# Attention plus channel-mixer block on one core: the load of the next head group's value weights is named after a unit's query stack pieces, its split one step later

## The chip, the cores and the metric

One Trainium2 chip, one of its cores. The metric is the device time of one execution of the whole program in microseconds (us). Three timed executions of the kernel before stand beside one that was profiled.

## The reference, cut to what matters

The input is 2048 tokens of width 1024, in float32. The first half of the block is a layer norm, an attention with 32 heads of width 32 that works through the sequence in four segments of 512 tokens with a running memory M, z, and a residual. The second half is a layer norm, a 1024 to 3584 to 1024 GELU network per token and another residual.

```
q, k, v = y @ wq, y @ wk, y @ wv            # y = layernorm(x), split into 32 heads, 4 segments
for s in range(4):
    p     = softmax(qs @ ks.T * scale + mask)
    a_dot = p @ vs
    a_mem = (phi(qs) @ M) / (phi(qs) @ z + 1e-6)
    o     = g * a_mem + (1 - g) * a_dot
    M, z  = M + phi(ks).T @ vs, z + sum(phi(ks))
h   = x + concat(o) @ wo
out = h + gelu(layernorm(h) @ w1 + b1) @ w2 + b2
```

## The kernel before, in words

Every product is made of float32 values split into a high part and a low remainder (`mm3`, lines 126 to 129: high by high, low by high, high by low), so a weight block comes from HBM as float32, is copied by VectorE or ScalarE to its high part, and GpSimd subtracts to give the low part.

The program runs twice over a half of 1024 tokens (two segments); the attention of each half comes first, the output projection and the mixer follow. The attention (`attention`, line 360) is cut into 16 **units** per half: a unit is one group of four heads (128 of the 1024 columns, so eight groups) and one segment. `ORDER` (lines 31 and 32) says which: groups 0 and 1 alternate in units 0 to 3, groups 2 to 5 take two units each, groups 6 and 7 alternate in units 12 to 15. The next unit has another head group after units 0, 1, 2, 3, 5, 7, 9, 11, 12, 13 and 14, and then its three weight blocks (q, k, v, of 512 KB each) must be fetched and split.

**Steps.** A unit is 24 steps, numbered from b = 24n. At step c TensorE does three matmuls of the unit's own projection: keys at c = 0 to 7, queries at 8 to 15, values at 16 to 23. After these, `close(step)` (line 678) runs the functions that were named for that step by `at(step, ...)`: in the order in which they were entered for it. A unit reaches over several later units: its logits start at step 22 (`QK1`, line 37), its second pass at 53, its product with the values at 71. The whole attention is recorded under `in_order()` (line 107), so each engine's instructions stand in exactly the order in which the steps name them, on SyncE's queue of transfers too. When an instruction must wait, all behind it on that engine wait as well.

**The stack pieces.** The logits need the high and low parts of four heads stacked on the partitions, (`stack`, line 414): three transfers of 64 KB for each of four heads j, for keys into `ks`, for queries into `qs`, all of them issued by SyncE. For the queries, ScalarE makes the high part `qq` at step b+15 (line 434), VectorE the low part at b+16 (line 440), and the pieces for j = 0 and 1 are named at b+17, for j = 2 at b+19, for j = 3 at b+24 (there right after the keys of j = 3). The first logits matmul of a unit (`qk1`, line 569) stands at b+22 and needs the three pieces of j = 0. VectorE reads its output (line 571), ScalarE takes the exponential one step later (line 573), and two PSUM banks take turns. "Query pieces 0 to 2" below are the nine transfers of j = 0, 1 and 2.

**The weights.** `wload` (lines 685 to 689) takes one of two raw buffers `wr` and issues the 512 KB load from SyncE (line 688). `wsplit` (lines 691 to 704) has VectorE copy the block to `wh` (line 695), and enters four pieces for the four steps behind it, in which GpSimd makes `wl` (line 699). The buffer is free when the fourth piece is done. Since there are two buffers, the load of v takes the one that k had in the same unit, and the next load of a k, q or v takes what is free. In units 1 to 14 that fetch weights the loads stand at b+2 (k), b+7 (q; b+13 in unit 1) and b+15 (v), the splits at b+9, b+17 and b+25.

Also on GpSimd in these steps: the causal cut of the exponentials `e` (line 626, `qk2`, named from step 53 on, which is b+5 to b+20 of a later unit and b+29 and on as seen from here), and the low part of the attention output (line 654, step 75).

Of the kernel before, what the change touches and what calls it, by code (L numbers as in the profile page):

```python
# [51 lines left out]
def build(tc, x, wq, wk, wv, wo, beta, w1, b1, w2, b2, out):  # L52
# [6 lines left out]
    def ps_dense(name):  # L59
        return psum.tile([P, 512], F32, tag="d", name=name, bufs=3)  # L60
# [16 lines left out]
    def constants():  # L77
        behind(nc.scalar.activation(bb, bb, AF.Exp, scale=-1.0))
        nc.scalar.activation(bb, bb, AF.Identity, bias=1.0)
        behind(nc.vector.reciprocal(gate[:, 0, :], bb))  # L80
        nc.scalar.activation(gate[:, 1, :], gate[:, 0, :], AF.Identity, scale=-1.0, bias=1.0)
        pb = ps_dense("pb")
        behind(nc.tensor.transpose(pb[:, :FB], b1r, ident[:FB, :FB]))
        nc.scalar.copy(b1c, pb[:, :FB])
        for j in range(4):
            b = slice(32 * j, 32 * j + 32)
            nc.gpsimd.tensor_copy(gcol[b, :], gate[b, 1, :].rearrange("p (g j) -> p g j", j=4)[:, :, j])
# [38 lines left out]
    def mm3(ps, ah, al, bh, bl, first, last):  # L126
        nc.tensor.matmul(ps, ah, bh, start=first, stop=False)  # L127
        nc.tensor.matmul(ps, ah, bl, start=False, stop=False)  # L128
        acts["mm"] = nc.tensor.matmul(ps, al, bh, start=False, stop=last)  # L129
# [230 lines left out]
    def attention(half, first):  # L360
# [15 lines left out]
        def at(step, *fns):  # L376
            assert step >= now[0], (step, now[0])
            todo.setdefault(step, []).extend(fns)
# [281 lines left out]
        def heads(u, b):  # L660
            for m, (j, i) in QK1.items():
                at(b + m, partial(qk1, u, j, i))
            at(b + QK0, partial(qk0, u))
            at(b + LSE, partial(lse, u))
            at(b + LSE + 1, partial(halves, u))
            at(b + TURN, partial(turn, u))
            for j, m in enumerate(ROWS):
                at(b + m, partial(rows, u, j))
            for m, (j, n) in QK2.items():
                at(b + m, partial(qk2, u, j, n))  # L670
            at(b + AV, partial(av, u))
            at(b + AV + 2, partial(out, u))
            at(b + AV + 3, partial(out_high, u))
            at(b + AV + 4, partial(out_low, u))
            if u["n"] < 13:
                at(b + AV + 6, partial(store, u))

        def close(step):

            now[0] = step  # L680
            for f in todo.pop(step, ()):
                f()
            one_small()
# [35 lines left out]
        for n in range(16):  # L719
            u = unit(n)  # L720
            heads(u, 24 * n)
            g, sl = ORDER[n]
            b = 24 * n
            if n < 15 and ORDER[n + 1][0] != g:
                g1 = ORDER[n + 1][0]
                for name, m, m1 in (("k", 2, 9), ("q", 7 if n > 1 else 13, 17), ("v", 15, 25)) if n else \
                        (("k", 14, 19), ("q", 17, 24), ("v", 24, 32)):
                    at(b + m, partial(wload, g1, name))
                    at(b + m1, partial(wsplit, g1, name, step=b + m1))
            if n == 14:  # L730
                for k, m in enumerate((1, 4, 8, 25, 27, 29, 41)):
                    at(b + m, partial(load_o, half, 0, k))
            if n == 15:
                wts, raws = acts["wts"], acts["raws"] = {}, {}

                def wo_load(k):
                    raws[0, k] = wo_raw(0, k)

                def wo_made(k, step):
                    wts[0, k], lows_ = wo_upper(raws.pop((0, k)), wo_home())  # L740
                    for i, f in enumerate(lows_):
                        at(step + 1 + i, f)

                for m, k in ((6, 0), (7, 1), (17, 2), (22, 3)):
                    at(b + m, partial(wo_load, k))
                for m, k in ((12, 0), (17, 1), (24, 2)):
                    at(b + m, partial(wo_made, k, b + m))
            acc = 0.0
            for c in range(24):
                name = "kqv"[c // 8]  # L750
                if c % 8 == 0:
                    u[name + "ps"] = ps_dense(name + "ps") if not (first and n == 0 and c == 0) else first["kps"]
                if first and n == 0 and c < 8:
                    if c == 7:
                        close(b + c)
                    continue
                w = first[name] if first and n == 0 else W[g, name]
                yh, yl = acts["y", sl]
                k = c % 8
                mm3(u[name + "ps"], w[0][:, k, :], w[1][:, k, :], yh[:, k, :], yl[:, k, :], k == 0, k == DC - 1)  # L760
                close(b + c)
                if side:
                    acc += 0.55 if half else 0.7
                    while acc >= 1.0:
                        acc -= 1.0
                        next(side, None)
            if n == 1:
                for _ in side:
                    pass
                side = None  # L770
                if first:
                    constants()
                acts.pop("last", None)
# [25 lines left out]
    def wo_raw(n, k):  # L799
        wr = wp.tile([P, DC, P], F32, tag="wr", name="wr", bufs=2).rearrange("p a b -> p (a b)").rearrange("p (c n) -> p c n", c=2)  # L800
        nc.sync.dma_start(wr, wo[k * 256:(k + 1) * 256, n * 512:(n + 1) * 512].rearrange("(c p) n -> p c n", p=P))
        return wr
# [6 lines left out]
    def wo_upper(wr, home):  # L809
        h, l = home  # L810
        nc.vector.tensor_copy(h, wr)

        def lower(i, c):
            c = slice(256 * c, 256 * c + 256)
            nc.gpsimd.tensor_tensor(l[:, i, c], wr[:, i, c], raw(h)[:, i, c], op=ALU.subtract)

        return home, [partial(lower, i, c) for i in range(2) for c in range(2)]

    def wo_home():
        return [wp.tile([P, DC, P], F32R, tag=t, name=t, bufs=3).rearrange("p a b -> p (a b)")  # L820
                .rearrange("p (c n) -> p c n", c=2) for t in ("wh", "wl")]
# [615 lines left out]
    for half in range(2):  # L1437
# [6 lines left out]
        order = ExitStack()  # L1444
        order.enter_context(in_order())
        rest = attention(half, first)
        next(rest)
        hts = [lnp.tile([P, D], F32, tag="ln", name="ht0", bufs=4) for _ in range(4)]
# [125 lines left out]
```

## Time and profile before

| | us |
|---|---|
| timed executions | 2183.11, 2184.59, 2187.11 |
| their median | 2184.59 |
| the profiled execution, its own time | 2187.23 |
| its span, first to last instruction | 2185.5 |
| TensorE busy in the span | 2157.7 |
| VectorE, ScalarE, GpSimd busy | 1349.0, 1102.1, 959.7 |

The profiled execution ran at the full granted TensorE clock. How to read it: a busy time is the sum of an engine's instructions, and an engine waits when an instruction that is next in its order needs something. A row of the timeline gives the start, the duration, the engine and line, what is written from what, and in brackets the idle time before it and who ended that. SPq is SyncE's queue, where a transfer's row is only its issue. Its landing is told by the view of transfers. Matmul rows overlap: a 128x512 matmul has about 0.39 us in the record, and the next may start 0.23 us after it started.

### The profile page before, as it was taken

To read this page: it belongs to the slowest core of one execution; us is meant where nothing else is said; L and a number is where in the kernel's file an instruction comes from. 1 tells how busy PE (TensorE), PEld (TensorE's weight loads), DVE (VectorE), ACT (ScalarE), POOL (GpSimd) and SP (SyncE) were. 2 spreads that over 40 slices of the span, in tenths; PEclk is the share of its full clock that TensorE was granted. 3 is DMA by queue.
4 is the path that set the end of the run, shared out by engine and by line. 5 is a ranking of instruction groups with operands and counts; after the bars stand their busy time and mean duration, and the time that the engine had idled before them with its cause. 6 is when DMAs were issued, how large, how long until landed. Compare 5 with 4: busy or idle time off the path is not lost.

```text
span 2185.5 us, 33210 instructions
## 1 busy us (share of the span) xinstructions
PE 2157.7 (99%) x10937; PEld 1750.4 (80%) x10937; DVE 1349.0 (62%) x2696; ACT 1102.1 (50%) x2433; POOL 959.7 (44%) x1206
## 2 busy tenths in 40 slices
PE   7999999999999999999999999999999999999999
PEld 6777777778888888877777768888887888888887
DVE  6766666665745556766667655745666665576653
ACT  5777777762543445777777752643443232322221
POOL 5534345562444434533335561534446544256330
PEclk9999999999999999999999999999999999999999
DMA  6544445664465655544444663575569865676762
GB/s 182 134 106 107 105 107 136 190 203 164 154 207 155 187 158 147 136 107 109 106 108 133 198 197 141 173 217 162 171 199 373 274 226 185 190 244 230 250 222 92
DMA packets 352405, 376.20 MB, mean 172 GB/s; under 512 B 27214, under 2 KB 244330, under 8 KB 352234
## 3 DMA queue, kind: packets, MB, share of 16 engines
q1 hardware_dynamic: 288778, 336.98, 50.7%
q10 hardware_dynamic: 63456, 37.10, 5.6%
q8 instruction: 87, 1.43, 0.3%
q14 instruction: 84, 0.69, 0.1%
HBM read 241.27 MB, written 82.38 MB: 148 GB/s over the span
## 4 chain that ended last, share of the span: by engine, by line
PE 91%; DVE 2%; DMA 2%; POOL 2%; ACT 1%; issue 1%; SPq 0%; ACTq 0%; DVEq 0%; POOLq 0%
PE po L1410 22%; PE bps L1014 10%; PE cps L1014 7%; PE dps L1014 7%; PE pst L619 4%; PE po L633 3%; PE pqk L569 3%; PE kps L127 3%; PE vps L127 3%; PE qps L127 3%; PE kps L128 3%; PE pwo L127 2%; PE kps L129 2%; PE vps L128 2%; PE pwo L129 2%; PE pwo L128 2%
## 5 line engine op out<-in xcount | busy, mean ns | idle before, releaser
L571 DVE CUSTOM_DVE_ANT_0 pqk<-pqk,mask 128x512 f32<-128x512 f32 (+2 forms) x384 | 216.9, 565 | 241.6 <-PE pqk L569 214.8
L573 ACT ACTIVATE junk<-pqk,mx 128x512 f32<-128x512 f32 (+2 forms) x384 | 225.2, 587 | 134.7 <-DVE mx L571 128.2
L626 POOL TENSOR_SCALAR_AFFINE_SELECT e<-e 128x128 f32<-128x128 f32 (+1 forms) x384 | 137.6, 359 | 268.9 <-ACT e L622 254.1
L699 POOL TENSOR_TENSOR wl<-wr,wh 128x256 fp32r<-128x256 f32 x268 | 202.1, 770 | 108.7 <-PE pqk L569 85.8
L622 ACT ACTIVATE e<-pst 128x384 f32<-128x384 f32 (+1 forms) x384 | 200.8, 529 | 70.9 <-PE pst L619 69.5
L1420 DVE TENSOR_TENSOR c<-c,po 128x512 f32<-128x512 f32 x160 | 105.4, 684 | 156.7 <-PE po L1410 153.9
L569 PE MATMUL pqk<-ks,qs 96*128 96x512 f32 (+2 forms) x384 | 138.6, 361 | 5.7 <-ACT junk L573 3.0
L619 PE MATMUL pst<-qs,ks 104*128 104x512 f32 (+3 forms) x512 | 140.9, 318 | 1.0 <-ACT e L622 0.4
L619 PEld LDWEIGHTS pst<-qs,ks 104*128 104x128 f32 x512 | 95.7, 188 | 34.7 <-ACT e L622 10.7
L1410 PE MATMUL po<-w2h,zh 128*128 128x512 f32 x378 | 120.9, 389 | 0.4 <-DVE zh L1350 0.4
L1267 POOL TENSOR_TENSOR w2r<-w2r 128x512 f32<-128x512 f32 x54 | 84.6, 1579 | 72.3 <-DMA w2r<-in_B_w 72.3
L127 PE MATMUL kps<-yh,wh 128*128 128x512 f32 (+1 forms) x264 | 113.5, 430 | 0.0
L127 PE MATMUL qps<-yh,wh 128*128 128x512 f32 x256 | 113.2, 442 | 0.0
L1014 PE MATMUL bps<-zh,sb 128*128 128x512 f32 x336 | 110.9, 391 | 0.0
L1014 PE MATMUL bps<-zh,sa 128*128 128x512 f32 x336 | 110.8, 390 | 0.0
L1126 POOL TENSOR_TENSOR s<-r 128x512 f32<-128x512 f32 x28 | 44.3, 1583 | 141.0 <-DVE sa L1142 81.3
L127 PE MATMUL vps<-yh,wh 128*128 128x512 f32 x256 | 105.0, 410 | 0.0
L1410 PE MATMUL po<-w2h,hl 128*128 128x512 f32 x322 | 103.2, 390 | 0.7 <-DVE hl L1350 0.4
L128 PE MATMUL kps<-yl,wh 128*128 128x512 f32 (+1 forms) x264 | 102.8, 389 | 0.5 <-DVE yl L165 0.4
L129 PE MATMUL kps<-yh,wl 128*128 128x512 f32 (+1 forms) x264 | 102.2, 387 | 0.0
L128 PE MATMUL qps<-yl,wh 128*128 128x512 f32 x256 | 101.0, 394 | 0.0
L128 PE MATMUL vps<-yl,wh 128*128 128x512 f32 x256 | 100.8, 394 | 0.0
(271 smaller groups left out, 6204.0 us busy)
## 6 DMA issues: line engine op xcount, KB each, us to landing
hr<-h_dram SPq DMA_DIRECT2D x112, 448.0 KB, 5.5
w2r<-in_B_w SPq DMA_DIRECT2D x122, 256.0 KB, 4.2
r<-in_B_w SPq DMA_DIRECT2D x56, 512.0 KB, 4.6
ks<-kk SPq DMA_DIRECT2D x360, 64.0 KB, 2.0
qs<-qq SPq DMA_DIRECT2D x360, 64.0 KB, 2.0
h_dram<-ht ACTq DMA_DIRECT2D x84, 256.0 KB, 3.6
wx<-in_B_w SPq DMA_DIRECT2D x56, 256.0 KB, 3.5
o_dram<-side SPq DMA_DIRECT2D x52, 256.0 KB, 4.2
```

Source lines behind the costliest of these rows:

```text
L127: nc.tensor.matmul(ps, ah, bh, start=first, stop=False)
L128: nc.tensor.matmul(ps, ah, bl, start=False, stop=False)
L129: acts["mm"] = nc.tensor.matmul(ps, al, bh, start=False, stop=last)
L569: nc.tensor.matmul(ps, u["qs"][0:96, j, i * P:(i + 1) * P], u["ks"][0:96, j, 0:n], start=True, stop=True)
L571: nc.vector.tensor_tensor_reduce(out=ps, in0=ps, in1=mask[:, 512 - n:512], op0=ALU.add, op1=ALU.min, scale=-SCALE, scalar=3.0e38, accum_out=m)
L573: at(now[0] + 1, lambda: nc.scalar.activation(acts["junk"][:, :n], ps, AF.Exp, bias=m, scale=-1.0, accum_out=u["mx"][:, 1, i, j:j + 1]))
L619: nc.tensor.matmul(ps[:, o:o + 512 - P * jk], u["ks"][:, j, jk * P:(jk + 1) * P], u["qs"][:, j, jk * P:512], start=True, stop=True)
L622: nc.scalar.activation(e, ps[:, :w], AF.Exp, scale=SCALE)
L626: nc.gpsimd.affine_select(d, d, pattern=[[0, 2], [1, P]] if n == 2 else [[1, P]], compare_op=ALU.is_ge, fill=0.0, base=0, channel_multipli ...
L699: nc.gpsimd.tensor_tensor(l[:, c], wr[:, c], raw(h)[:, c], op=ALU.subtract)
L1014: nc.tensor.matmul(ps, x_[:, c, :], y_[:, c, :], start=first and c == 0 and n == 0, stop=last and c == 3 and n == 2, skip_group_check=True)
L1410: nc.tensor.matmul(ps, x_[:, k], y_[k], start=opens and k == 0 and i == 0, stop=closes and k == self.KP - 1 and i == 2, skip_group_check=True)
```

## The change: what it does

The load of v moves from step b+15 to b+21, and its split from b+25 to b+26, in units 1 to 14 where the next unit has another head group: 10 units per half (1, 2, 3, 5, 7, 9, 11, 12, 13, 14), 20 in all. Unit 0, which has its own steps, stays.

```diff
             if n < 15 and ORDER[n + 1][0] != g:
                 g1 = ORDER[n + 1][0]
-                for name, m, m1 in (("k", 2, 9), ("q", 7 if n > 1 else 13, 17), ("v", 15, 25)) if n else \
+                for name, m, m1 in (("k", 2, 9), ("q", 7 if n > 1 else 13, 17), ("v", 21, 26)) if n else \
                         (("k", 14, 19), ("q", 17, 24), ("v", 24, 32)):
                     at(b + m, partial(wload, g1, name))
                     at(b + m1, partial(wsplit, g1, name, step=b + m1))
```

Three engines get another order. On SyncE's queue the load of v (`wr<-in_A_wv`) stood ahead of the query pieces of its unit, in the fence below in a unit of the first half:

```order
 L688 DMA wr<-in_A_wq 128x8x128
 L417 DMA ks_179<-kk 32x512 x6
-L688 DMA wr<-in_A_wv 128x8x128
 L417 DMA qs_181<-qq 32x512 x6
 L417 DMA ks_179<-kk 32x512 x3
 L417 DMA qs_181<-qq 32x512 x3
+L688 DMA wr<-in_A_wv 128x8x128
 L417 DMA ks_179<-kk 32x512 x3
 L417 DMA qs_181<-qq 32x512 x3
```

It now stands behind the query pieces of j = 0, 1 and 2 and the key pieces of j = 2: twelve transfers later, ahead of the pieces of j = 3.

On VectorE the copy to the high part (`wh<-wr`, line 695) moves behind one logits tile (line 571, two rows), in a unit whose two-unit-older neighbour has its output scaled just ahead (line 644):

```order
 L571 ISA mx 128x1
 L644 TENSOR_SCALAR side<-po,few 128x512
-L695 CAST wh<-wr 128x1024
-L571 ISA pqk,mx<-pqk,mask 128x256
-L571 ISA mx 128x1
+L571 ISA pqk,mx<-pqk,mask 128x256
+L571 ISA mx 128x1
+L695 CAST wh<-wr 128x1024
 L469 SCALAR_TENSOR_TENSOR rg<-pm,bb 128x2x4
 L472 RECIPROCAL rg<-rg 128x2x4
```

It now stands right ahead of the reads of the memory product (lines 469 and 472), and the logits tile of step b+26 no longer stands behind it.

On GpSimd the four pieces of v's low part (`wl<-wr,wh`, line 699) each stand one step later. Before, in a stretch that starts with the last three pieces of q's and the first of v's:

```order
L699 TENSOR_TENSOR wl<-wr,wh 128x256 x4
L654 TENSOR_TENSOR side<-side 128x512
L699 TENSOR_TENSOR wl<-wr,wh 128x256 x2
L626 AFFINE_SELECT e<-e 128x128
L699 TENSOR_TENSOR wl<-wr,wh 128x256
L626 AFFINE_SELECT e<-e 128x128
L626 AFFINE_SELECT e<-e 128x256
```

And now, the same stretch:

```order
L699 TENSOR_TENSOR wl<-wr,wh 128x256 x3
L654 TENSOR_TENSOR side<-side 128x512
L699 TENSOR_TENSOR wl<-wr,wh 128x256 x2
L626 AFFINE_SELECT e<-e 128x128
L699 TENSOR_TENSOR wl<-wr,wh 128x256
L626 AFFINE_SELECT e<-e 128x128
L699 TENSOR_TENSOR wl<-wr,wh 128x256
L626 AFFINE_SELECT e<-e 128x256
```

The attention output's low part (line 654) goes ahead of all four of v's pieces, and the fourth goes behind one more cut of `e`. TensorE and ScalarE keep their order.

## The prediction

> **What bounds the kernel now.** I read the page first, then who TensorE waits for, then SyncE's own waits and the view of transfers, and last the timeline around the two waits. The page's first part and the line on TensorE's waits:
>
> ```profile
> PE 2157.7 (99%) x10937; PEld 1750.4 (80%) x10937; DVE 1349.0 (62%) x2696; ACT 1102.1 (50%) x2433; POOL 959.7 (44%) x1206
> ...
> PE pqk L569 <- DMA qs<-qq: 2.4, 2, 1.3
> ```
>
> TensorE is the bound, 99% busy, and other engines have slack. What this change can win must be idle time of TensorE that ends with query stack pieces: 2.4 us, in two waits, the longest 1.3 us. SyncE's queue waits far more at the weight loads (line 688), for GpSimd, and transfers to landing have very different lengths:
>
> ```profile
> SPq L688 <- POOL e L626: 70.5, 25, 3.7
> SPq L688 <- POOL wl L699: 20.9, 13, 3.8
> ...
> qs<-qq SPq DMA_DIRECT2D x360, 64.0 KB, 2.0
> ...
> wr<-in_A_wv SPq DMA_DIRECT2D x24, 512.0 KB, 4.3
> ```
>
> A stack piece lands 2.0 us after its issue at the median, a v block 4.3. In time order, here is the first of the two waits (unit 1 of the first half):
>
> ```profile
> 56.02 0.59 ACT L434 CAST qq<-qps 128x512 fp32r<-128x512 f32 x1 [1.49 <-PE qps L129]
> 57.56 0.69 DVE L440 TENSOR_TENSOR qq<-qps,qq 128x512 fp32r<-128x512 f32 x1
> 58.19 0.37 SPq L688 DMA_DIRECT2D wr<-in_A_wv  x1
> 58.66 3.71 SPq L417 DMA_DIRECT2D qs<-qq  x6
> 61.84 0.40 PE L129 MATMUL vps<-yh,wl 128*128 128x512 f32 x1
> 63.52 0.47 PE L569 MATMUL pqk<-ks,qs 96*128 96x512 f32 x1 [1.28 <-DMA qs<-qq]
> ```
>
> The high part `qq` was done at 56.61, but the pieces were issued only from 58.66, behind a v load that SyncE could not issue before 58.19. The second (unit 7):
>
> ```profile
> 221.54 0.39 PE L129 MATMUL vps<-yh,wl 128*128 128x512 f32 x1
> 221.61 0.58 ACT L434 CAST qq<-qps 128x512 fp32r<-128x512 f32 x1
> 221.77 0.39 PE L569 MATMUL pqk<-ks,qs 96*128 96x512 f32 x1
> 221.86 0.39 SPq L688 DMA_DIRECT2D wr<-in_A_wv  x1
> 222.34 5.05 SPq L417 DMA_DIRECT2D qs<-qq  x6
> 222.82 0.69 DVE L440 TENSOR_TENSOR qq<-qps,qq 128x512 fp32r<-128x512 f32 x1
> 226.85 0.39 PE L129 MATMUL vps<-yh,wl 128*128 128x512 f32 x1
> 228.37 0.47 PE L569 MATMUL pqk<-ks,qs 96*128 96x512 f32 x1 [1.13 <-DMA qs<-qq]
> ```
>
> Here the issue was only 0.14 us behind `qq` (222.19 to 222.34); the transfers were late. The view of transfers for this stretch, and the landings of these pieces (shortest, median, longest):
>
> ```profile
> wr<-in_A_wv SPq DMA_DIRECT2D x1, 512.0 KB, 4.6
> qs<-qq SPq DMA_DIRECT2D x6, 64.0 KB, 4.0
> ...
> DMA to landing us min/median/max: 3.4/4.0/4.5
> ```
>
> Pieces behind a v block take 4.0 us instead of 2.0: they wait for it on the transfer engines. Most units have about 2 us to spare there, which is why only two of the 20 moved places show a wait.
>
> **The change part by part.** *The load leaves the pieces' way.* In unit 1 they can be issued from 56.61, the third piece (the low part, ready at 58.25) at about 58.3; with 2.0 us they land by 60.3, before TensorE comes to them at about 62.1. In unit 7 the third is issued when the low part is done (223.51), and with the longest landing of 4.5 it was there at about 228.0; with the median of 2.0 it is there at 225.5, and TensorE comes at 227.1 (226.85 and 0.23). Both waits go. In starts of matmuls: from a line-129 matmul to a logits matmul it is 0.23 us where nothing waits (221.54 to 221.77); it was 1.68 (61.84 to 63.52) and 1.52 (226.85 to 228.37). So 1.45 + 1.29 = 2.74 us go, a little more than the idle record, because records of matmuls overlap. What is late next in unit 7 is nothing: the windows from the first logits matmul of one unit to that of the next, which end at the moved units 7 (with the wait at 228.37) and 9 (without one; the second figure is TensorE's busy time),
>
> ```profile
> 200.40:228.40 28.00, 26.80 (x158) 20.96 (x156) 17.11 (x50) 20.68 (x58) 11.60 (x23) 1.00 0.49 130
> 256.40:283.00 26.60, 26.54 (x157) 21.05 (x156) 16.52 (x50) 19.94 (x55) 10.79 (x21) 1.00 0.52 138
> ```
>
> show 26.80 of 28.00 and 26.54 of 26.60. A moved unit without such a wait has next to nothing to give, and nothing else idles near unit 7 that would take back what is won.
>
> *The load issues later.* It now follows twelve pieces. The place is where the pieces of j = 3 start, in unit 3 at 120.25:
>
> ```profile
> 112.17 0.39 SPq L688 DMA_DIRECT2D wr<-in_A_wv  x1
> ...
> 120.25 3.02 SPq L417 DMA_DIRECT2D ks<-kk  x3
> 123.49 0.69 DVE L695 CAST wh<-wr 128x1024 fp32r<-128x1024 f32 x1
> 124.16 0.43 DVE L571 CUSTOM_DVE_ANT_0 pqk<-pqk,mask 128x256 f32<-128x256 f32 x1
> 125.01 1.29 POOL L654 TENSOR_TENSOR side<-side 128x512 fp32r<-128x512 f32 x1
> 125.31 0.17 DVE L469 SCALAR_TENSOR_TENSOR rg<-pm,bb 128x8 f32<-128x8 f32 x1 [0.66 <-PE pm L408]
> 126.81 0.68 DVE L571 CUSTOM_DVE_ANT_0 pqk<-pqk,mask 128x512 f32<-128x512 f32 x1
> 128.46 0.73 POOL L699 TENSOR_TENSOR wl<-wr,wh 128x256 fp32r<-128x256 f32 x1
> 128.58 0.20 ACT L573 ACTIVATION_READ_ACCUMULATOR junk<-pqk,mx 128x1 f32 x1
> 130.69 0.28 PE L569 MATMUL pqk<-ks,qs 96*128 96x256 f32 x1
> 130.71 0.41 POOL L626 TENSOR_SCALAR_AFFINE_SELECT e<-e 128x256 f32<-128x256 f32 x1 [1.17 <-ACT e L622]
> ```
>
> The load itself has no wait there, its buffer has long been read. Issued at about 120.2, it lands at 124.5 by the median of 4.3. The copy `wh` now stands behind the tile of 124.16 and can start at about 124.6 (124.16 and 0.43): level with the landing. Costed at nothing: the copy takes the place where VectorE sat idle for 0.66 us ahead of line 469, ends at about 125.3, and all behind it stays. *If the landing is late*, VectorE waits at the copy, and behind it stand lines 469 to 473, a row copy (line 610) and the tile of 126.81. Its reader on ScalarE ended at 128.78 (128.58 + 0.20), and the matmul that needs that bank again starts at 130.69: 1.9 us of cover. Up to a landing at 126.5, or 6.3 us from the issue, the price is nothing; beyond, one us per us.
>
> The longest landing of any weight load of line 688 was 8.0 us:
>
> ```profile
> DMA to landing us min/median/max: 3.6/4.3/8.0
> ```
>
> [...]
>
> *GpSimd.* Four pieces per unit, each a step later; the order is in the fences above. The output's low part (125.01, 1.29) goes first, then two pieces, a cut, a piece, a cut, and the fourth ends some 1.1 us later than 129.19, before the cut of 130.71. Nothing of it is on TensorE's path. Its one follower is the next unit's q load on SyncE (or the raw load of the projection weights), which is issued 1 us later, with the next unit's key pieces behind it; those are named 13 steps of 1.17 us (28.00 by 24) ahead of their reader, 15 us, of which one us is no loss. So 0, and at most some tenths if a transfer there is late as well.
>
> Sum: -2.7 us against the profiled execution's own 2187.23, so 2184.5. That execution was 2.64 over the median of the timed ones, which spread from 2183.11 to 2187.11. I take the sum off the median: 2184.59 - 2.7 = **2181.9**. What a measurement here can tell from no change is about 0.2%, or 4.4 us: the faster side begins at 2180.2, the slower at 2189.0.
>
> **The rivals.** *Nothing changes (chance 0.15).* The wait at 63.52 might only hide the next one: soon after, TensorE waits for the low part of the next segment's layer norm, and with 1.45 us less lead that wait could grow by as much, and the late transfers of unit 7 may be an accident of one execution. Time 2184.6. Against it stands the timeline's row of that layer norm,
>
> ```profile
> 64.47 0.59 ACT L163 CAST yh<-pt 128x512 fp32r<-128x512 f32 x1 [2.53 <-PE pt L161]
> ```
>
> ScalarE itself waited 2.53 us for TensorE there, so the chain moves up with it. For it: the whole gain is smaller than the spread of the runs.
>
> *VectorE waits at the copy (0.09), slower.* If landings take the 8.0 us of the longest in all 20 units, each is 1.7 us past the cover: 34 us less 2.7, 2216. It decides from 6.3 us on; slower by 4.4 needs 7.1 us net, 0.36 us in each unit, so landings of about 6.7. For it: the load now shares the queue with six pieces and, in units 12 to 14, with loads of the attention's outputs just behind it. Against it: those are issued behind it, and the 4.3 is a median of loads with pieces behind. The tightest place is unit 1 of the second half, where the copy stood at 883.88:
>
> ```profile
> 882.76 1.85 SPq L417 DMA_DIRECT2D ks<-kk  x3
> 883.88 0.69 DVE L695 CAST wh<-wr 128x1024 fp32r<-128x1024 f32 x1
> ```
>
> Issued at about 882.4 it lands at 886.7, and behind the tile ahead of it VectorE waits some 1.6 us, just inside the 1.9, if the cover is the same there.
>
> *More than the two waits (0.08), faster.* Unprofiled executions may have more such waits: 20 places run with the pieces 2 us late, and each that slips costs about 1.3. Five of them instead of two give 6.5 us, 2178.1. Against it: the windows of the other units are full.
>
> *The load isn't out of the way (0.03):* the pieces could be held by something else ahead of them; then 2184.6. The order shows only key pieces ahead.
>
> **How the numbers follow.** The forecast has 0.65. It and the two cases without change give what lies within 0.2%, less the share of the forecast that the runs' spread of 4 us puts below 2180.2 (about a tenth). Faster 0.08 and 0.05: 0.13. Slower 0.08: the slower rival, less the part in which only few units wait. Same 0.79. The range leaves out a tenth on each side: from 2179.3 (the forecast less the lower half of the spread and a third wait) to 2186.8 (no change, the upper half of the spread).
>
> **What would show it right or wrong.** Right: no wait of TensorE for `qs<-qq`, pieces 0 landing in 2.0 us in moved units, the load in unit 3 issued near 120 and the copy near 124.6. Wrong: a wait of VectorE for `wr<-in_A_wv` of over 2 us with one of TensorE for ScalarE's exponentials behind it, or the same waits for `qs` at the same units, or a median beyond 4.4 us on either side.

## The result and the profile after

The changed kernel took 2209.14 us at the median of 5 runs (2205.3 to 2209.3), the kernel before 2184.59 beside it (2183.11 to 2189.91): a ratio of 1.0102 [1.0089, 1.0116], slower by 1.0%, some 22 us. The forecast was 2181.9 within 2179.3 to 2186.8. Of the eleven runs of e3 below, one of 3137.14 us, at a granted clock of 0.64, is left out of its median and its ratio.

The profiled execution of the changed kernel took 2209.3 us with a span of 2207.6, against 2185.5 before: 22.1 us more. First its page, part 1. TensorE is still the bound. Its busy time has grown by 4.9 us, and the other 17.2 are idle time.

```profile
PE 2162.6 (98%) x10937; PEld 1754.7 (79%) x10937; DVE 1365.6 (62%) x2696; ACT 1100.6 (50%) x2433; POOL 952.9 (43%) x1206
```

Next the view of waits of the changed kernel: who waits for whom, us in total, times, the longest.

```profile
ACT qs L610 <- DVE qs L610: 58.5, 32, 4.5
PEld pst L619 <- ACT e L622: 33.6, 33, 3.5
PE pst L619 <- ACT e L622: 20.6, 22, 3.1
DVE wh L695 <- DMA wr<-in_A_wv: 20.1, 18, 3.3
```

The same view of the kernel before:

```profile
ACT qs L610 <- DVE qs L610: 35.1, 32, 1.5
PEld pst L619 <- ACT e L622: 10.7, 31, 0.6
PE pst L619 <- ACT e L622: 0.4, 2, 0.2
```

TensorE's matmuls of the second pass (line 619) now wait 20.6 us for ScalarE's exponentials (line 622), where they waited 0.4. ScalarE waits 23.4 us more for VectorE's row copy (line 610), and VectorE waits 20.1 us for the v block. The chain from the block to TensorE can be read from bottom to top. The wait for `qs<-qq` that the change was about (2.4 us before) is gone from the view.

The transfers, with the median from issue to landing, and the landings of all loads of line 688 (shortest, median, longest) in the changed kernel:

```profile
wr<-in_A_wv SPq DMA_DIRECT2D x24, 512.0 KB, 4.5
```

```profile
DMA to landing us min/median/max: 3.7/4.6/6.7
```

The first row is the v blocks alone, the second all loads of weights. The median of the v blocks is 4.5, where the forecast took 4.3: the load itself did not become much slower. The place of the first old wait, unit 1 of the first half, in the timeline of the changed kernel:

```profile
56.36 4.05 SPq L417 DMA_DIRECT2D qs<-qq  x6
...
61.60 0.40 PE L129 MATMUL vps<-yh,wl 128*128 128x512 f32 x1
61.84 0.40 PE L569 MATMUL pqk<-ks,qs 96*128 96x512 f32 x1
```

The pieces start at 56.36 instead of 58.66, and the logits matmul stands 0.24 us behind the line-129 matmul: no wait.

**Where the time went.** Windows from the first logits matmul of a unit to that of the next, in the changed kernel, for units 3 and 5 (length; then busy time and count of PE, PEld, DVE, ACT, POOL; granted clock, DMA share, GB/s):

```profile
117.66:146.90 29.24, 28.03 (x170) 22.42 (x169) 17.72 (x56) 19.39 (x55) 10.78 (x22) 1.00 0.36 91
173.56:202.28 28.72, 28.05 (x170) 22.43 (x169) 18.46 (x55) 19.70 (x57) 11.26 (x24) 1.00 0.36 95
```

The same two units before:

```profile
117.85:145.78 27.93, 27.93 (x169) 22.41 (x168) 17.37 (x55) 19.41 (x55) 10.84 (x23) 1.00 0.31 77
172.44:200.39 27.95, 27.95 (x170) 22.42 (x168) 17.71 (x55) 19.68 (x57) 11.24 (x24) 1.00 0.31 78
```

TensorE had no idle time in either before. Unit 3 now loses 1.31 us and unit 5 0.77. The units in which the change moves nothing keep their length (unit 4 is 26.66 in both). Two things happen. In unit 3 the block lands late; the timeline of the changed kernel:

```profile
119.94 1.69 SPq L688 DMA_DIRECT2D wr<-in_A_wv  x1
...
123.96 0.43 DVE L571 CUSTOM_DVE_ANT_0 pqk<-pqk,mask 128x256 f32<-128x256 f32 x1 [0.58 <-PE pqk L569]
...
124.13 1.29 POOL L654 TENSOR_TENSOR side<-side 128x512 fp32r<-128x512 f32 x1 [4.72 <-ACT side L651]
...
125.83 0.69 DVE L695 CAST wh<-wr 128x1024 fp32r<-128x1024 f32 x1 [1.38 <-DMA wr<-in_A_wv]
...
127.32 0.68 DVE L610 CAST qs<-ptn 8x512 fp32r<-8x512 f32 x1
...
128.04 0.57 ACT L610 CAST qs<-ptn 8x512 fp32r<-8x512 f32 x1 [2.80 <-DVE qs L610]
...
128.64 0.60 ACT L622 ACTIVATE e<-pst 128x512 f32<-128x512 f32 x1
...
129.29 0.44 PE L619 MATMUL pst<-qs,ks 104*128 104x384 f32 x1 [1.21 <-ACT e L622]
```

And the same steps before, in the same unit, with two rows of VectorE ahead of them:

```profile
125.51 0.20 DVE L472 RECIPROCAL rg<-rg 128x8 f32<-128x8 f32 x1
...
125.75 0.42 DVE L473 TENSOR_TENSOR om<-pm,rg 128x256 f32<-128x256 f32 x1
...
126.20 0.68 DVE L610 CAST qs<-ptn 8x512 fp32r<-8x512 f32 x1
...
126.92 0.57 ACT L610 CAST qs<-ptn 8x512 fp32r<-8x512 f32 x1 [1.48 <-DVE qs L610]
...
127.52 0.60 ACT L622 ACTIVATE e<-pst 128x512 f32<-128x512 f32 x1
...
128.17 0.45 PE L619 MATMUL pst<-qs,ks 104*128 104x384 f32 x1
```

The row copies of j = 1 (VectorE) and j = 2 (ScalarE, which waits for the first), the exponential behind them in ScalarE's order, and the matmul that needs its bank follow each other with gaps of 0.05 us and less already before: 126.20 + 0.68, 126.92 + 0.57, 127.52 + 0.60, 128.17. On VectorE, lines 469 to 473 stand end to end ahead of the first row copy, from 125.31 on (the prediction has that row). TensorE did not wait there, and had no cover either. Now VectorE waits 1.38 us for the block ahead of the copy `wh`, and the whole chain moves, to the matmul.

In unit 5 of the changed kernel the block was there in time, and the copy itself is long:

```profile
180.03 1.29 POOL L654 TENSOR_TENSOR side<-side 128x512 fp32r<-128x512 f32 x1 [4.24 <-ACT side L651]
180.34 1.53 DVE L695 CAST wh<-wr 128x1024 fp32r<-128x1024 f32 x1
...
182.67 0.68 DVE L610 CAST qs<-ptn 8x512 fp32r<-8x512 f32 x1
...
184.64 0.44 PE L619 MATMUL pst<-qs,ks 104*128 104x384 f32 x1 [0.67 <-ACT e L622]
```

It takes 1.53 us instead of 0.69, beside GpSimd's low part of the output (line 654), and ends 0.55 us behind that. Before, the copy stood one logits tile earlier and had ended when line 654 began (124.18 against 125.01 in unit 3). In GpSimd's order of before, line 654 stood behind a low piece of v that reads that copy, so the two could not meet.

### The profile page after: what moved, and what is told of

Same layout as the page of the kernel before. It is cut to its first block, busy times and chain, and to the rows that moved or that the text cites. A ratio compares the mean times of both kernels' runs of the same rounds, so it can differ in the third digit from the quotient of the medians.

```text
span 2207.6 us, 33200 instructions
## 1 busy us (share of the span) xinstructions
PE 2162.6 (98%) x10937; PEld 1754.7 (79%) x10937; DVE 1365.6 (62%) x2696; ACT 1100.6 (50%) x2433; POOL 952.9 (43%) x1206
## 4 chain that ended last, share of the span: by engine, by line
PE 87%; DMA 4%; DVE 3%; SPq 2%; ACT 2%; issue 1%; POOL 1%; DVEq 0%; POOLq 0%; ACTq 0%
PE po L1410 23%; PE bps L1014 10%; PE cps L1014 7%; PE dps L1014 7%; PE pst L619 3%; PE pqk L569 3%; PE po L633 3%; PE qps L127 3%; PE pwo L127 2%; DMA wr<-in_A_wv 2%; PE pwo L128 2%; PE qps L128 2%; PE pwo L129 2%; PE qps L129 2%; SPq L417 2%; PE vps L127 2%
## 5 line engine op out<-in xcount | busy, mean ns | idle before, releaser
L619 PE MATMUL pst<-qs,ks 104*128 104x512 f32 (+3 forms) x512 | 141.5, 319 | 21.0 <-ACT e L622 20.6
L129 PE MATMUL qps<-yh,wl 128*128 128x512 f32 x256 | 101.4, 396 | 0.0
```

The source lines that it names most:

```text
L619: nc.tensor.matmul(ps[:, o:o + 512 - P * jk], u["ks"][:, j, jk * P:(jk + 1) * P], u["qs"][:, j, jk * P:512], start=True, stop=True)
```

## Experiments

Two theories stood against each other. **Theory 1**: the loss is the late load; VectorE waits for the block. **Theory 2**: the loss is the later split; the copy runs beside GpSimd's line 654. Later a third question came up: by which way a delay of VectorE reaches TensorE (theory A, through the row copies; its rival B, that VectorE has cover there). All kernels are the kernel before with the edit shown. The kernel before stood at a median of 2186.44 us beside the first four, and at 2186.85 beside the last four.

**e1_split_only**: the load stays, only the split goes one step later.

```diff
-("v", 15, 25)
+("v", 15, 26)
```

> The split of v one step later (b+26), its load where it was (b+15). Theory 1 (the load lands too late, and only that costs): the block has landed long before, so no loss, 2184.6 within 2. Theory 2 (the copy now runs beside GpSimd's low part of the attention output, line 654, which takes 1.29 us, and VectorE's copy can't end before that one has; 1.53 us instead of 0.69 in the changed kernel's unit 5): about 0.75 us in each of some 18 moved units, 13 to 15 us, so about 2199, with copies of about 1.5 us in the trace and no wait for a transfer at them. The waits for query pieces stay in both.

Measured: 2200.02 us (2197.27 to 2201.31, 4 runs), ratio 1.0058 [1.0044, 1.0072]. All copies of line 695 (shortest, median, longest in ns) and unit 5 in its timeline:

```profile
L695 DVE CAST wh<-wr x66: 682/689/1676, 31.6 to 1249.8; 128x1024 fp32r<-128x1024 f32 x66
```

```profile
178.42 1.29 POOL L654 TENSOR_TENSOR side<-side 128x512 fp32r<-128x512 f32 x1 [4.51 <-DMA qs<-qq]
...
178.60 1.66 DVE L695 CAST wh<-wr 128x1024 fp32r<-128x1024 f32 x1
...
181.77 0.57 ACT L610 CAST qs<-ptn 8x512 fp32r<-8x512 f32 x1 [2.24 <-DVE qs L610]
...
183.02 0.45 PE L619 MATMUL pst<-qs,ks 104*128 104x384 f32 x1 [0.67 <-ACT e L622]
```

With the load where it was, one step of the split costs 0.6% by itself. The copy takes 1.66 us beside line 654, and TensorE waits 0.67 us. In 18 of the 20 moved units the copy takes 1.65 to 1.68 us; the 12.7 us of the ratio are some 0.7 for each of the 18, and unit 5 is 28.75 us long (171.87 to 200.62) where it was 27.95.

**e2_load_only**: the load goes later, the split stays.

```diff
-("v", 15, 25)
+("v", 21, 25)
```

> The load of v at b+21, its split where it was (b+25), so that the copy stands ahead of a logits tile and GpSimd's line 654 behind v's first low piece. Theory 1 (late landing): the copy waits until 6.5 to 8.3 us after the unit's first logits matmul, and the tile, the row copy and ScalarE's exponential all behind it: at least the loss of the change, 20 to 30 us, 2205 to 2215. Theory 2 (line 654 alone): the order has the copy done before line 654 can start, so no loss beyond the landing; if the landing were harmless, 2182 to 2185.

Measured: 2215.53 us (2212.58 to 2217.89, 4 runs), ratio 1.013 [1.0116, 1.0144]. What VectorE waited for ahead of line 695, and its copies:

```profile
L695 DVE CAST wh<-wr x66: 682/689/696, 33.7 to 1268.1; 128x1024 fp32r<-128x1024 f32 x66
...
  DMA wr<-in_A_wv: 43.6, 22
```

No copy is stretched, but VectorE waits 43.6 us for the block, in 22 places. So the load alone costs more than the change does: the copy stands one logits tile earlier here, so the same landing is later for it, and the tile waits behind it. Theory 1 has a loss of its own too, and the question is what the two make together (e5).

**e3_load17**: the load goes behind the six pieces of j = 0 and 1 only, the split stays.

```diff
-("v", 15, 25)
+("v", 17, 25)
```

> The load of v at b+17, behind the six query pieces of j = 0 and 1 only, its split at b+25 as before. Both theories: the query pieces are free of the block (their waits of 2.4 us go), the block is issued about 1.5 us ahead of the unit's first logits matmul and lands 3 us behind it, over 2 us ahead of the copy; GpSimd's order is as before. So 2.7 us less than before, 2181.9, within the noise of no change. If it is slower by over 5 us, neither theory is complete.

Measured: 2183.09 us at the median of 10 runs (2179.47 to 2185.23), ratio 0.9982 [0.9973, 0.9991], and no wait of TensorE for `qs<-qq`. 0.18% of 2186 is 3.9 us, with an interval of 2.0 to 5.9, in which the 2.7 us that the forecast counted for the two waits lie. So the gain is there, if the block is still in time for its copy.

**e4_split_low_later**: the split one step later as in e1, and GpSimd's low part of the output with its store three steps later, so that they no longer meet.

```diff
-("v", 15, 25)
+("v", 15, 26)
...
-            at(b + AV + 4, partial(out_low, u))
+            at(b + AV + (7 if u["n"] < 13 else 4), partial(out_low, u))
             if u["n"] < 13:
-                at(b + AV + 6, partial(store, u))
+                at(b + AV + 9, partial(store, u))
```

> As the split alone one step later (load at b+15, split at b+26), but GpSimd's low part of the attention output (line 654) is named three steps later, and its store too, so it is not beside the copy any more. Theory 2: the loss of the split alone goes, 2184.6 within 3, copies of 0.69 us. Theory 1: no loss in either. If it stays at 2195 or more, the place of the copy behind the logits tile costs by itself and line 654 has nothing to do with it.

Measured: 2185.02 us (2184.11 to 2188.7, 10 runs), ratio 0.9995 [0.9986, 1.0005]: the loss of e1 is gone. Unit 5 in its timeline:

```profile
177.53 0.69 DVE L695 CAST wh<-wr 128x1024 fp32r<-128x1024 f32 x1
...
182.15 1.30 POOL L654 TENSOR_TENSOR side<-side 128x512 fp32r<-128x512 f32 x1
```

The copy takes 0.69 us again. That the loss of the split is the meeting with line 654 is shown.

**e5_both_low_later**: the change itself, with line 654 out of the way as in e4.

```diff
-("v", 15, 25)
+("v", 21, 26)
```

> The change whole (load at b+21, split at b+26), with GpSimd's line 654 and its store named three steps later, so that only the late landing is left. If the two causes run side by side (the copy ends by whichever lets it go last), each unit loses what its landing alone makes late: from the changed kernel's trace, copies that start at 6.7 to 8.5 us for a place at 6.8, about 16 us in all, 2198 to 2203. If line 654 was the main cost, 2184 to 2190. If the costs add up, the split's 13 us go from the change's 24: 2194 to 2197.

Measured: 2202.18 us (2201.02 to 2204.92, 4 runs), ratio 1.0073 [1.0059, 1.0087]. This is the price of the landing alone, some 16 us by the ratio (that line 654 costs nothing in its new place was seen in e4); the split alone cost 12.7 (e1), both together 22. They do not add up, since the copy waits for both at once: in unit 3 of the changed kernel line 654 had ended at 125.42 when the copy began at 125.83, so only the block counted there.

**e6_vector_delay**: how much cover VectorE has in that place. The kernel before, with two instructions on VectorE in the moved units behind the logits tile of step b+26, whose results nobody reads (1.28 us for the two). Lines behind the edit are numbered one higher.

```diff
+        idle = few[:, 40:52]
...
+                if n:
+                    for k in range(2):
+                        at(b + 26, partial(nc.vector.bn_stats, idle[:, 6 * k:6 * k + 6], mask))
```

> The kernel before with nothing moved, and two bn_stats of the mask (0.63 us each, output unused) on VectorE at step b+26 of the 20 moved units, behind the logits tile: a delay of VectorE with no transfer and no GpSimd in it. 0.66 us of it fall in VectorE's wait for the memory product. Theory A (no cover: VectorE's row copy, ScalarE's next row copy and the first exponential of the second pass lead straight to TensorE): some 0.6 us in each unit, 11 to 13 us, 2196 to 2199. Theory B (1.9 us of cover, as the prediction had it): 2184.6 within 3.

Measured: 2196.18 us (2193.99 to 2200.47, 4 runs), ratio 1.0049 [1.0031, 1.0068]. Unit 5 in its timeline:

```profile
182.51 0.57 ACT L611 CAST qs<-ptn 8x512 fp32r<-8x512 f32 x1 [1.86 <-DVE qs L611]
...
183.11 0.60 ACT L623 ACTIVATE e<-pst 128x512 f32<-128x512 f32 x1
183.76 0.44 PE L620 MATMUL pst<-qs,ks 104*128 104x384 f32 x1 [0.29 <-ACT e L623]
```

No transfer and no GpSimd instruction is moved here, and the same chain moves and ends in the same wait. VectorE hides there its idle time of 0.66 us ahead of line 469 and little beyond: of the 1.28 us, 0.41 come out in unit 5 (28.36 us from 172.98 to 201.34, against 27.95), and the ratio gives 10.7 us (6.8 to 14.9) for the 20 units, some 0.5 each. Rival B, with 1.9 us of cover, would have shown no loss from 1.28 us.

**e7_both_row_scalar**: the change itself, with the row copy of j = 1 on ScalarE, in all units.

```diff
-("v", 15, 25)
+("v", 21, 26)
...
-            (nc.vector.tensor_copy if j % 2 else nc.scalar.copy)(u["qs"][96:KX, j, :], u["pt"][0:8, :])
+            (nc.vector.tensor_copy if j == 3 else nc.scalar.copy)(u["qs"][96:KX, j, :], u["pt"][0:8, :])
```

> The change whole, and in all 32 units the row copy of j = 1 (line 610) goes to ScalarE, so that ScalarE's row copy of j = 2 and the first exponential no longer wait for VectorE. Theory A (the loss comes through that row copy): what is left is the other way, through the logits tile, which has cover for about 1 us; most of the loss goes, 2183 to 2190. Theory B (the loss comes through the logits tile and its exponential): no less than 2200. ScalarE gets 32 copies of 0.57 us more, which could cost by themselves; the run beside it tells.

Measured: 2183.59 us (2182.62 to 2186.24, 10 runs), ratio 0.9987 [0.9978, 0.9996]. What VectorE waits for ahead of line 695, and unit 3 in the timeline:

```profile
L695 DVE CAST wh<-wr x66: 682/687/1656, 33.0 to 1239.1; 128x1024 fp32r<-128x1024 f32 x66
...
  DMA wr<-in_A_wv: 17.6, 18
```

```profile
124.70 1.05 ACT L610 CAST qs<-ptn 8x512 fp32r<-8x512 f32 x2
124.99 0.69 DVE L695 CAST wh<-wr 128x1024 fp32r<-128x1024 f32 x1 [1.10 <-DMA wr<-in_A_wv]
...
126.69 0.60 ACT L622 ACTIVATE e<-pst 128x512 f32<-128x512 f32 x1 [0.93 <-PE pst L619]
```

VectorE still waits 17.6 us for the block, and its copy still meets line 654, yet the whole loss is gone: both row copies are done at 125.75, and the exponential waits for TensorE instead of the other way round. The edit also takes 0.68 us of work off VectorE in each unit, which gives the other way, through the logits tile, more room; but in the changed kernel the wait stands at the exponentials behind the row copies, and in e6 too, where VectorE was only delayed. The three together show the way through the row copies.

**e8_load17_row_scalar**: the load as in e3, and the row copy of j = 1 on ScalarE.

```diff
-("v", 15, 25)
+("v", 17, 25)
...
-            (nc.vector.tensor_copy if j % 2 else nc.scalar.copy)(u["qs"][96:KX, j, :], u["pt"][0:8, :])
+            (nc.vector.tensor_copy if j == 3 else nc.scalar.copy)(u["qs"][96:KX, j, :], u["pt"][0:8, :])
```

> The load of v at b+17 with its split at b+25, and the row copy of j = 1 on ScalarE in all 32 units: what the moved row copy costs or brings where nothing is late. Against the load at b+17 alone (2183.9, 2.6 below the kernel before beside it): the first exponential stands at best 0.1 us earlier in each unit, 0 to 3 us less, 2181 to 2184; if ScalarE is short there, some us more, 2186 to 2190.

Measured: 2181.69 us (2180.68 to 2185.56, 11 runs), ratio 0.998 [0.9971, 0.9989]. It beats both kernels, as e3 does (0.9982), and the two can't be told apart: once the block lands in time, the row copy's place is worth nothing measurable.

## Why the prediction was wrong, step by step

**Right: the two waits go.** The pieces of unit 1 were issued from 56.36 (forecast 56.61), the wait at 63.52 is gone, and so is that of unit 7. Unit 7's six pieces of j = 0 and 1 now land at a median of 2.1 us from their issue (1.9 to 2.9), where it was 4.0 behind the block; there the view of transfers of before, in slices of 0.175 us, has the busy share of the transfer engines at nine tenths or more from 223.95 to 225.88. In e3, where nothing else is lost, the ratio is 0.9982, and the forecast's 2.7 us lie in its interval.

**Right: the load's place and its landing.** In unit 3 it was issued at 119.94 (forecast: about 120.2), and the median landing was 4.5 us (taken: 4.3). Landings past 6.3 us from the issue, on which the slower rival was built, did not come: the longest of a v block that the trace has is the 5.8 of unit 3.

**Wrong, the step that decided: the cover.** "The load issues later" was costed at nothing with "1.9 us of cover", up to a landing 6.3 us from the issue. The prediction named what stands behind the copy on VectorE (lines 469 to 473, a row copy, the tile of 126.81), and then followed only the last of these to its readers: tile, exponential of line 573, logits matmul at 130.69. The row copy in the same list leads to TensorE by a shorter way, and that way had no cover at all, as the rows of before in the first section show. What VectorE could give was its idle time of 0.66 us ahead of line 469, and the copy itself, 0.69 us long, used that up. By those rows the copy had to start at 124.62 in unit 3 (125.31 less 0.69), 4.4 us behind an issue at 120.2: a median landing of 4.3 leaves 0.1 us, not 1.9. In 18 places VectorE waited for the block (16 of them in moved units, 2 in unit 0, which has its own steps), and what it was late beyond the cover came out at TensorE; e6 and e7 show this way, e5 its price of some 16 us. It is also what the prediction had named as a sign of being wrong: a wait of VectorE for the block with one of TensorE for the exponentials behind it. The slower rival had the right mechanism with a threshold that lay 1.9 us too late, and so 0.09 for what came.

**Wrong in the same step: the tightest place.** In unit 1 of the second half the prediction expected the issue at 882.4, that is 1.66 us behind the unit's first logits matmul (880.74 before), and some 1.6 us of waiting, "just inside the 1.9". It was issued 2.76 us behind that matmul (889.37 in the changed kernel), and the copy waited 3.28:

```profile
892.13 0.53 SPq L688 DMA_DIRECT2D wr<-in_A_wv  x1
...
896.92 0.69 DVE L695 CAST wh<-wr 128x1024 fp32r<-128x1024 f32 x1 [3.28 <-DMA wr<-in_A_wv]
```

TensorE then waited 3.11 us at line 619 (900.38), and this unit alone grew by 4.74 us, more than units 3, 5 and 13 of the first half (1.31, 0.77 and 3.08 us).

**Wrong: GpSimd at nothing.** "Nothing of it is on TensorE's path" looked at where GpSimd's instructions end. It did not ask what runs beside them. The prediction quoted the row of line 654 at 125.01 for 1.29 us, and set the copy at 124.6 to 125.3, so the meeting stood in its own rows. Line 654 began earlier than that in the changed kernel (124.13 in unit 3), and the copy was stretched to 1.53 to 1.66 us in the three moved units whose block was in time, and by less in some others: 0.77 us in unit 5, 0.6% of the kernel where all blocks are in time (e1), nothing when the two are kept apart (e4). In both rows of the meeting line 654 keeps its 1.29 us and the copy ends 0.55 us behind it: in e1 line 654 runs from 178.42 to 179.71 and the copy from 178.60 to 180.26, in unit 5 of the changed kernel line 654 from 180.03 to 181.32 and the copy from 180.34 to 181.87. By what the one holds up the other, no run here shows.

**The sum.** By the view of waits, TensorE lost 20.2 us more at line 619 (20.6 less 0.4) and won the 2.4 at the query pieces. Three falls of the clock (the last section) cost some 1.7 us each. That makes 22.9 us, against the 22.1 by which the span grew. The third fall, 1.7 us, is not put down to the change.

**The price of the late issue.** In unit 3 before, 11.32 us lay between the issue of the load (112.17) and its copy (123.49), and the median landing of 4.3 us left 7 of them to spare. In the changed kernel 5.89 us lie between them (119.94 to 125.83), and VectorE waited in 1.38 of these for the block. The prediction put this price at nothing, by a cover that was not there. Why the block landed 5.8 us behind the issue in unit 3 and 4.0 in unit 5 stays open. The issue itself took 1.69 us in unit 3, and 0.53 in unit 5, which may be part of it, but no run took that apart.

## What to carry to other kernels

When an instruction on a side engine moves or may wait, follow every instruction queued behind it to its readers on the engine that is the bound, and take the way with the least room: a row "X waits for Y: 0.0" with three instructions end to end behind it means no cover, not no dependence. Ask also what will run beside the moved instruction, on VectorE and GpSimd above all, since the copy of 0.69 us became one of 1.66 beside line 654 (e1). And a transfer that is in the way of others need only go behind those that are waited for (six pieces, e3), not behind all that share its queue.

## What the runs showed of the hardware

A wait of TensorE can cost more than its length. In unit 13 of the changed kernel TensorE waits 1.72 us; in unit 3 it waited 1.21. The windows of the 5 us behind each (the third column from the end is the granted clock), behind the wait of 3.11 us at 900.38, and from 1300.19, near the end of the second half's attention:

```profile
129.29:134.29 5.00, 5.00 (x29) 4.43 (x30) 3.34 (x12) 4.22 (x11) 2.70 (x6) 1.00 0.06 13
408.06:413.06 5.00, 5.00 (x19) 4.21 (x20) 1.83 (x6) 3.05 (x8) 2.40 (x5) 0.66 0.91 280
900.38:905.38 5.00, 5.00 (x19) 4.28 (x20) 2.03 (x7) 3.11 (x8) 2.40 (x5) 0.66 0.34 98
...
1300.19:1305.19 5.00, 4.97 (x18) 4.16 (x19) 1.78 (x4) 3.16 (x11) 1.70 (x4) 0.66 0.97 328
```

Behind the 1.72 and the 3.11 the clock falls to 0.66 over 5 us, so by estimate 0.34 by 5, some 1.7 us, are lost once more each time: 3.4 us in all, and these two units lost 3.08 and 4.74 us. The third fall, at 1300, has no such wait ahead of it: the matmul at 1300.19 waited 0.72 us, and in the 5 us from 1295 to 1300 TensorE was idle for 0.72. Its cause stays open. The change need not be in it: the profiled execution of the kernel before has no fall up to 2184 us and a mean granted clock of 1.000, but of its 21 executions beside e1 to e4 ten have a mean of 0.998 or 0.999, and so has the profiled one of e4 (0.999), which is not slower. By estimate, one fall of 1.7 us in 2185 makes 0.999. Three falls are some 5.1 us, close to the 4.9 by which TensorE's busy time grew.

In e2 the same was seen (0.66 over 5 us) behind waits of 1.75, 2.00 and 3.42 us, in e5 behind one of 3.74, but in e2 not (1.00) behind waits of 1.67 and of 1.82. The rows of e2 for the 1.82 and the 1.75:

```profile
297.78:302.78 5.00, 5.00 (x29) 4.42 (x30) 3.33 (x12) 4.22 (x11) 2.25 (x6) 1.00 0.17 56
382.14:387.14 5.00, 5.00 (x19) 4.28 (x20) 1.47 (x6) 3.05 (x8) 2.68 (x6) 0.66 0.58 192
```

So at 1.7 to 1.8 us it can go either way, and the length of one wait does not decide it alone. No fall is seen in the 5 us behind the wait of 8.75 us at the start of the changed kernel either (1.00 from 8.75 to 13.75). The shortest of these waits with a fall behind it is that of 1.72 us, and the third fall stands behind 0.72 us of idle time. What sets off a fall, no run here shows.
